# A gated MLP on one Trainium2 core: raw weight rows of the down projection fetched two steps sooner and, in the first pass, ahead of the last three stores, with loads of sums and of the next x begun later

## Chip, cores and metric

The kernel runs on one core of one Trainium2 chip. The metric is the device time of one execution in microseconds. A profiled execution also gives the span, from the first to the last instruction, which is about 2 us shorter.

## The reference

```python
# x: [1, 2048, 1024], w_gate, w_up: [1024, 3584], w_down: [3584, 1024], all bf16
g = jnp.einsum("bsd,df->bsf", x, w_gate)
u = jnp.einsum("bsd,df->bsf", x, w_up)
h = _gelu(g) * u
return jnp.einsum("bsf,fd->bsd", h, w_down)
```

## The kernel before

The 2048 rows of x are done in two passes of 1024. A pass has an up phase (14 units that produce the hidden tile `hT`) and a down projection. Both use 7 instead of 8 block products, after Winograd's form of Strassen's scheme, so the down projection needs sums of blocks of w_down as well as raw blocks. In the first pass each unit makes the sums of one row block of w_down on the side and stores them to a scratch tensor `td` in DRAM; the last unit makes three. The down projection then reads them back.

The down projection is written as numbered steps. An agenda says at which step each load is put on the queue; at each step TensorE does four or eight matmuls. All these loads and stores are issued by one engine, SP, in program order. The steps do not gate SP by time: they only fix the order of its instructions. SP waits when an instruction's data or buffer is not ready, and then everything behind it waits too.

```python
AT12 = [2, 2, 5, 5, 8, 8, 16, 18, 20, 22, 27, 29, 31, 33]   # steps of the loads of sums
...
def store_made(j):                      # 0.75 MB: three sums of row block j
    nc.sync.dma_start(out=td[:, j], in_=made[j][:, :3].bitcast(f32))
...
def load12(j):
    if j in BIG12:                      # (0, 2, 4): two blocks' sums in one 1 MB load
        big = wpool.tile([P, 2, 2, N], f32, name="w")
        nc.sync.dma_start(out=big, in_=td[:, j : j + 2, :2])
        ...
    elif j - 1 not in BIG12:            # 6 to 13: two loads of 256 KB
        ...
def fetch12(n):                         # 256 KB: one raw row tile, enough for 8 matmuls
    kh, j = n // 7, 2 * (n % 7)
    rl = slot([P, 2, N], bf16, "raw")
    nc.sync.dma_start(out=rl, in_=wdn[:, kh, j : j + 2, :N])
    raw[1, n] = rl
...
for n in range(NJ):                     # NJ = 14
    at(max(-1, 2 * n - 6), fetch12, n)
...
# down projection, phase one: steps 0 to 27, four bf16 matmuls each
for kh in range(2):
    ...
    for j in range(NJ):
        step(kh * NJ + j)
        rl = raw[1, kh * 7 + j // 2]
        rows((e, c)[kh], hT[:, kh, j, 0, :], rl[:, j % 2, :], j == 0, j == NJ - 1)
# phase two reads the sums (q12), from step 28
...
# in each unit of the up phase (js: the row blocks whose sums it makes; the last unit has three)
if js:
    store_made(js[0])
for j in js[1:]:
    keep_whole(j)
...
def more(step):                         # beside the first down projection
    if step in (-1, 1):
        store_made(NJ - 2 + (step > 0))
    ...
    if step >= 16 and step % 2 == 0 and step // 2 - 8 < len(moves):
        c, ko = moves[step // 2 - 8]
        transposing(xT, c, ko, (2 * (ip + 1) + c) * N)      # the next pass's x
```

I call the fourteen tiles of `fetch12` rows 0 to 13, and "big loads" the three 1 MB loads of sums.

## Time and profile before

The median of the first three runs was 549.08 us (548.2 to 550.6). The page of the profiled execution (548.68 us, span 546.8) says what bounds it. In its lines, PE is TensorE; the digits are tenths in 40 equal slices of the span; the last line is the chain of waits that ended last, by engine.

```profile
span 546.8 us, 7414 instructions
...
PE 536.2 (98%) x2405; PEld 378.7 (69%) x2405; DVE 341.3 (62%) x526; ACT 258.4 (47%) x463; POOL 236.2 (43%) x212
...
PEclk9999999999999999999999999999999999999999
...
PE 92%; DMA 5%; SPq 2%; DVE 0%; issue 0%; ACT 0%; DVEq 0%; ACTq 0%
...
```

TensorE is busy 98% of the span at full clock, so time can be won only where it stands. Who waited for whom, TensorE alone; the columns are the sum in us, the number of waits and the longest:

```profile
engine line waited for: us in total, times, longest us
PE bank L111 <- DMA raw<-in_w_down_dram: 4.6, 4, 1.4
PE bank L494 <- DVE warm L428: 1.2, 1, 1.2
PE bank L111 <- DMA xT<-in_x_dram: 0.9, 2, 0.6
PE bank L444 <- DMA xn<-in_x_dram: 0.5, 1, 0.5
```

The three small entries belong to the first 21 us of the program. The rest is the first line: 4.6 us in four waits for raw rows. The timeline of TensorE shows where they are (start, us from the first start to the last end, operation, count; in brackets the idle time listed before the group and what ended it):

```profile
start us, us, engine line op out<-in xcount [idle before <-releaser]
...
184.45 1.97 PE L111 MATMUL bank<-t,sa 128*128 128x512 f32 x8
187.73 8.79 PE L111 MATMUL bank<-raw,hT 128*128 128x512 bf16 x40 [1.31 <-DMA raw<-in_w_down_dram]
197.88 1.89 PE L111 MATMUL bank<-raw,hT 128*128 128x512 bf16 x8 [1.35 <-DMA raw<-in_w_down_dram]
201.20 3.61 PE L111 MATMUL bank<-raw,hT 128*128 128x512 bf16 x16 [1.43 <-DMA raw<-in_w_down_dram]
205.28 10.52 PE L111 MATMUL bank<-raw,hT 128*128 128x512 bf16 x48 [0.47 <-DMA raw<-in_w_down_dram]
215.45 0.81 PE L111 MATMUL bank<-w,q 128*128 128x512 f32 x2
```

The up phase ends with the group of 184.45; then come the 112 matmuls of phase one, held before rows 0, 5, 6 and 8 (8 matmuls a row). At 215.45 phase two begins. (In some of the traces shown further on a few matmul records are missing, so that their counts add up to a little less than 112.)

Why the rows are late is told by the same stretch on SP's queue (start, us, issue, count):

```profile
171.64 1.52 SPq L261 DMA_DIRECT2D w<-in_w_down_dram  x3
181.89 0.33 SPq L280 DMA_DIRECT2D td<-m  x1
182.31 2.62 SPq L329 DMA_DIRECT2D raw<-in_w_down_dram  x3
185.03 0.45 SPq L280 DMA_DIRECT2D td<-w  x1
185.53 0.42 SPq L329 DMA_DIRECT2D raw<-in_w_down_dram  x1
186.05 1.22 SPq L280 DMA_DIRECT2D td<-w  x1
187.36 1.55 SPq L329 DMA_DIRECT2D raw<-in_w_down_dram  x1
188.96 1.29 SPq L290 DMA_DIRECT2D w<-td  x1
190.30 1.26 SPq L329 DMA_DIRECT2D raw<-in_w_down_dram  x1
...
```

SP issued nothing from 173.16 to 181.89: it stood at the store of the first kept sum, until DVE had made it. Behind that store the rows, two more stores and the three big loads alternate; the lines left out at the end go on in the same way, with the second and third big load behind rows 5 and 7. The stretch in which TensorE waits, with the share and speed of the DMA engines in the last two columns:

```profile
core 0: us, PE busy (x) PEld busy (x) DVE busy (x) ACT busy (x) POOL busy (x), PEclk, DMA share, GB/s
186.20:210.20 24.00, 19.43 (x88) 8.59 (x88) 19.04 (x30) 2.05 (x4) 0.00 (x0) 1.00 1.07 369
```

### The profile page before, as it was taken

Reading aid. Unit: us, or ns where it says so; the run is one execution under the profiler, and the core shown is the slowest. Engines: PE = TensorE matmul, PEld = TensorE weight load, DVE = VectorE, ACT = ScalarE, POOL = GpSimd, SP = SyncE. Lnnn points to the kernel's source line nnn. Section 1 sums busy time; section 2 is a strip of 40 time slices with the busy share of each in tenths; the row PEclk is TensorE's granted clock in tenths of the full one; section 3 lists DMA queues with packets and bytes.
Section 4 is the critical chain, followed back from the end, with each engine's and each line's share of the span. In section 5 each row is a group of like instructions: output and inputs, shape, how many; then the busy total and the mean of one; then the engine's idle time right before and its main releaser. Section 6 shows DMA issues by size and latency. Waiting matters only on the chain.

```text
span 546.8 us, 7414 instructions
## 1 busy us (share of the span) xinstructions
PE 536.2 (98%) x2405; PEld 378.7 (69%) x2405; DVE 341.3 (62%) x526; ACT 258.4 (47%) x463; POOL 236.2 (43%) x212
## 2 busy tenths in 40 slices
PE   8999999999999979999999999999999999999997
PEld 5477777667767635888877766776777775478885
DVE  3886766766666893585955555455555449766730
ACT  2466666566656410155445555555555551114431
POOL 0069966677774300000087777777777600000000
PEclk9999999999999999999999999999999999999999
DMA  8776666667645699999745222222222059373751
GB/s 210 168 199 174 173 180 203 197 179 208 199 146 173 229 383 289 308 197 276 263 134 135 78 79 77 78 77 79 77 78 77 0 199 381 133 230 97 226 187 49
DMA packets 108133, 93.28 MB, mean 171 GB/s; under 512 B 17216, under 2 KB 92992, under 8 KB 108096
## 3 DMA queue, kind: packets, MB, share of 16 engines
q1 hardware_dynamic: 103936, 90.72, 56.3%
q10 hardware_dynamic: 4160, 2.10, 1.5%
q8 instruction: 19, 0.31, 0.2%
q14 instruction: 18, 0.15, 0.1%
HBM read 74.45 MB, written 15.20 MB: 164 GB/s over the span
## 4 chain that ended last, share of the span: by engine, by line
PE 92%; DMA 5%; SPq 2%; DVE 0%; issue 0%; ACT 0%; DVEq 0%; ACTq 0%
PE bank L111 92%; DMA raw<-in_w_down_dram 3%; SPq L448 2%; DMA xT<-in_x_dram 1%; DMA xn<-in_x_dram 1%; DVE m L90 0%; SPq L437 0%; ACT bank L269 0%; ACT st L408 0%; SPq L280 0%; ACT u L107 0%; DVEq L90 0%; SPq L329 0%; ACTq L107 0%
## 5 line engine op out<-in xcount | busy, mean ns | idle before, releaser
L93 POOL TENSOR_TENSOR s<-w 128x512 fp32r<-128x512 bf16 x100 | 117.0, 1190 | 191.6 <-DVE t L90 92.8
L111 PE MATMUL bank<-t,s 128*128 128x512 f32 x648 | 157.0, 398 | 0.0
L111 PEld LDWEIGHTS bank<-t,s 128*128 128x128 f32 x648 | 121.8, 188 | 27.7
L111 PE MATMUL bank<-xT,w 128*128 128x512 bf16 (+1 forms) x504 | 116.5, 377 | 0.9 <-DMA xT<-in_x_dram 0.9
L107 ACT COPY p<-bank 128x512 f32<-128x512 f32 x124 | 70.4, 591 | 96.7 <-PE bank L111 96.7
L90 DVE TENSOR_TENSOR hT<-g,bank 128x512 bf16<-128x512 f32 x112 | 76.6, 687 | 54.7 <-ACT g L178 48.9
L111 PEld LDWEIGHTS <-w 128*128 128x128 bf16 x504 | 45.1, 98 | 60.3 <-issue 14.9
L90 DVE TENSOR_TENSOR sum<-bank,p 128x512 f32<-128x512 f32 x54 | 37.4, 692 | 53.2 <-PE bank L111 47.9
L178 ACT ACTIVATE g<-sum 128x512 f32<-128x512 f32 x81 | 51.5, 635 | 32.9 <-DVE sum L90 32.0
L111 PE MATMUL bank<-q 128*128 128x512 f32 x240 | 58.9, 389 | 0.0
L111 PE MATMUL bank<-t,sa 128*128 128x512 f32 x216 | 58.6, 413 | 0.0
L93 POOL TENSOR_TENSOR s<-w,s 128x512 fp32r<-128x512 bf16 x50 | 57.8, 1177 | 0.0
L93 POOL TENSOR_TENSOR s<-s,w 128x512 fp32r<-128x512 f32 x50 | 57.1, 1165 | 0.0
L111 PE MATMUL bank<-raw,hT 128*128 128x512 bf16 x224 | 49.2, 379 | 4.6 <-DMA raw<-in_w_down_dram 4.6
L111 PE MATMUL bank<-tb,s 128*128 128x512 f32 x216 | 53.3, 389 | 0.0
L111 PEld LDWEIGHTS bank<-q 128*128 128x128 f32 x240 | 45.1, 188 | 9.3
L111 PEld LDWEIGHTS bank<-t,sa 128*128 128x128 f32 x216 | 40.7, 188 | 10.6
L111 PEld LDWEIGHTS bank<-tb,s 128*128 128x128 f32 x216 | 40.6, 188 | 8.4
L102 ACT CAST tb<-raw 128x512 fp32r<-128x512 bf16 x28 | 17.2, 627 | 60.5 <-DMA raw<-in_w_down_dram 24.5
L107 ACT COPY u<-bank 128x512 f32<-128x512 f32 x62 | 35.9, 590 | 20.9 <-PE bank L111 19.2
L111 PEld LDWEIGHTS <-hT 128*128 128x128 bf16 x224 | 21.8, 98 | 31.6 <-issue 6.0
L90 DVE TENSOR_TENSOR bank<-bank,p 128x512 f32<-128x512 f32 x54 | 37.8, 700 | 8.2 <-PE bank L111 5.0
(44 smaller groups left out, 459.1 us busy)
## 6 DMA issues: line engine op xcount, KB each, us to landing
raw<-in_w_down_dram SPq DMA_DIRECT2D x80, 256.0 KB, 4.9
q<-td SPq DMA_DIRECT2D x60, 256.0 KB, 4.8
w<-in_w_gate_dram SPq DMA_DIRECT2D x25, 512.0 KB, 5.6
w<-in_w_up_dram SPq DMA_DIRECT2D x25, 512.0 KB, 6.5
td<-m SPq DMA_DIRECT2D x12, 768.0 KB, 4.6
w<-td SPq DMA_DIRECT2D x6, 1024.0 KB, 8.8
out_dram<-st SPq DMA_DIRECT2D x32, 128.0 KB, 1.7
td<-w SPq DMA_DIRECT2D x2, 768.0 KB, 6.7
```

The source lines that it names most:

```text
L90: nc.vector.tensor_tensor(out=out, in0=a, in1=b, op=op)
L93: nc.gpsimd.tensor_tensor(out=out, in0=a, in1=b, op=op)
L102: nc.scalar.copy(out=t, in_=src)
L107: nc.scalar.copy(out=t, in_=ps)
L111: nc.tensor.matmul(ps, lhsT=lhs, rhs=rhs, start=start, stop=stop, skip_group_check=True)
L178: nc.scalar.activation(g, src, ACT.Gelu_apprx_tanh)
L448: nc.sync.dma_start_transpose(out=xT[c][:, ko, :], in_=x2[r0 : r0 + N, ko * P : (ko + 1) * P])
```

## The change

Its intent is to bring the raw rows to TensorE in time. No compute is added or removed. Four things move on SP's queue: the last unit's store goes behind the first rows ("order"); rows are fetched two steps sooner ("sooner"); the three big loads begin 4 to 6 steps later ("sums"); and the next x begins 8 steps later ("x"). "Sooner" and "sums" change the agenda of both passes, but TensorE had no wait for rows in the second pass.

```diff
-    AT12 = [2, 2, 5, 5, 8, 8, 16, 18, 20, 22, 27, 29, 31, 33]
+    AT12 = [6, 6, 10, 10, 14, 14, 16, 18, 20, 22, 27, 29, 31, 33]
@@
-        at(max(-1, 2 * n - 6), fetch12, n)
+        at(max(-1, 2 * n - 8), fetch12, n)
@@
-                if js:
+                if len(js) == 1:
                     store_made(js[0])
@@
-            if step in (-1, 1):
-                store_made(NJ - 2 + (step > 0))
+            if step in (-1, 0, 2):
+                store_made({-1: NJ - 3, 0: NJ - 2, 2: NJ - 1}[step])
@@
-            if step >= 16 and step % 2 == 0 and step // 2 - 8 < len(moves):
-                c, ko = moves[step // 2 - 8]
+            if step >= 24 and step % 2 == 0 and step // 2 - 12 < len(moves):
+                c, ko = moves[step // 2 - 12]
```

## The prediction

> **What bounds the kernel now.** TensorE: PE is busy 98% of the 546.8 us span at full granted clock (busy table, clock row), and the chain of waits is 92% PE. After the first microseconds PE stands still for data in one place only: the start of the first down projection. The waits of PE list 4.6 us in 4 waits on the raw w_down rows: 1.31 us before 187.73, 1.35 before 197.88, 1.43 before 201.20 and 0.47 before 205.28 (timeline, 182 to 215 us). The second down projection and all other phases show no such gap. So at most 4.6 us, 0.84% of the time, can be won.
>
> **Why the rows are late.** The SP queue issues in order. Its last w_down load of the up phase ends at 173.16; then it stands 8.7 us at the store of the first kept sum, until DVE has made it (181.89). Only then do rows 0 to 2 issue; row 0 lands at 187.69, while PE is ready at 186.4. Thereafter the queue is full: from 186.4 to 216.0 it moves 364 GB/s at full DMA share (windows), and three 0.75 MB stores and three 1 MB loads of sums stand between the rows, each 2 to 3 us of queue. A 256 KB row alone takes 0.65 to 0.75 us of it. Rows landed 5.4 us after issue at first, 10.7 in the thick of it. Landings come in the order of issue, as the Trainium skill says of descriptors on one ring (DMA: Bandwidth & Descriptors, Queues, rings and completion order); the trace agrees.
>
> **What the change moves.** No instruction is added or removed; the compute engines keep their order. On SP four rows now stand before the first of the three stores, and rows 4 and 5 between them; the three big loads of sums come after rows 7, 9 and 11 instead of 4, 5 and 7. The buffers of rows 0 to 3 are those of before; their last readers, by the timeline, end between 171.8 and 175.7, so I expect issues from 173.2 to about 177 and landings (4.5 to 5 us after, as the loads of 169 to 173 show) by 182, in a time in which DMA is idle. Stacking the rest at the paces above (estimate from the landings of before), row 4 lands near 188 (needed 193.5), row 8 near 197 (200.6), row 10 near 201 (204.2), row 12 near 205 (207.8), row 13 near 207 (209.5): each tile feeds PE 1.78 us, and the slack stays above 2 us. All four gaps should go.
>
> **Given back.** The next x begins 8 steps later, so two transposes (1.14 us of SP each) now stand before the next weights at about 249 us. Those weights landed at 255.6 and 257.2, and DVE used them at 259.4, held by PE; slack about 1 to 2 us after the delay. If used up, DVE's stores push PE's fourth phase: perhaps 0.5 us.
>
> **Predicted.** 549.1 - 4.5 = 544.6 us, range 543.3 to 546.8. Faster by over 2%: 0.01; within 2%: 0.98; slower: 0.01.
>
> **What would show it.** Waits of PE: no or nearly no entry for raw rows; first raw matmul near 186.4 instead of 187.73, phase one 24.9 us instead of 29.6 long, everything later 4.5 us earlier with PE busy unchanged. Rows 0 to 3 issued before 178. No new PE gap around 255 to 265.
>
> **What would make it wrong.** A row buffer freed later than I read, holding the queue at row 1 or 2 and with it the stores; the loads of sums landing after 211 us; the late transposes holding up weights or sums; a gap hidden under another wait (banks freed by DVE at 186) that remains when the rows come early.

## The result, and the profile after

The changed kernel took 543.35 us (median of 4 runs, 542.67 to 543.71). Beside it the kernel before took 549.5 us (4 runs, 548.2 to 550.6; the three runs told of above are among them). A ratio in this document is the mean time of one kernel's runs over that of the other's of the same rounds, so not quite the ratio of the medians: here 0.9887, with a 95% interval of 0.9862 to 0.9912. That is 6.2 us of 549.4, where 4.5 had been forecast. Taken on the 549.08 us that the prediction started from, it is 542.9 us, 0.4 us below the lower end of its range.

The page after, the same lines (span, engines, granted clock, chain):

```profile
span 541.5 us, 7420 instructions
...
PE 535.2 (99%) x2405; PEld 378.0 (70%) x2405; DVE 341.6 (63%) x526; ACT 258.1 (48%) x463; POOL 236.5 (44%) x212
...
PEclk9999999999999999999999999999999999999999
...
PE 95%; SPq 2%; DMA 1%; issue 0%; ACT 0%
...
```

The waits of TensorE after:

```profile
engine line waited for: us in total, times, longest us
PE bank L494 <- DVE warm L428: 1.2, 1, 1.2
PE bank L111 <- DMA xT<-in_x_dram: 1.1, 1, 1.1
PE bank L444 <- DMA xn<-in_x_dram: 0.2, 1, 0.2
```

The entry for raw rows is gone. TensorE's timeline runs through phase one in a single group, from 186.21, 1.5 us sooner than before, to phase two at 210.21, 5.2 us sooner:

```profile
184.39 1.97 PE L111 MATMUL bank<-t,sa 128*128 128x512 f32 x8
186.21 24.35 PE L111 MATMUL bank<-raw,hT 128*128 128x512 bf16 x112
210.21 6.04 PE L111 MATMUL bank<-w,q 128*128 128x512 f32 x25
```

SP's queue after has four rows in the stretch in which it stood before, and the stores and big loads behind more rows (the second and third big load, in the lines left out, come behind rows 9 and 11):

```profile
173.21 3.76 SPq L329 DMA_DIRECT2D raw<-in_w_down_dram  x4
181.84 0.34 SPq L280 DMA_DIRECT2D td<-m  x1
182.28 0.38 SPq L329 DMA_DIRECT2D raw<-in_w_down_dram  x1
182.74 0.91 SPq L280 DMA_DIRECT2D td<-w  x1
183.74 0.84 SPq L329 DMA_DIRECT2D raw<-in_w_down_dram  x1
184.68 1.70 SPq L280 DMA_DIRECT2D td<-w  x1
186.48 2.40 SPq L329 DMA_DIRECT2D raw<-in_w_down_dram  x2
188.93 1.26 SPq L290 DMA_DIRECT2D w<-td  x1
...
```

The same 24 us window. The DMA engines move as much as before, but TensorE is now busy in all of it:

```profile
186.20:210.20 24.00, 24.00 (x113) 10.91 (x113) 19.07 (x31) 2.05 (x4) 0.00 (x0) 1.00 1.01 368
```

Three lengths make the comparison exact. "Start" is the time of the last matmul start of the up phase; "phase one" runs from there to the first matmul start of phase two; "rest" runs from there to the end of the last compute instruction (a ScalarE copy; the span ends 2.8 us after it with semaphore instructions).

| us | start | phase one | rest |
|---|---|---|---|
| before | 186.04 | 29.41 | 328.53 |
| after | 185.98 | 24.23 | 328.50 |

So the whole difference of these two traces is 5.2 us in phase one. The start of the program moved between 185.0 and 186.4 us over all fourteen profiles, with no relation to the variant: the first loads take a little more or less. That is chance that the span carries.

### The profile page after: what moved, and what is told of

Same layout as the page of the kernel before. It is cut to its first block, busy times and chain, and to the rows that moved or that the text cites. A ratio compares the mean times of both kernels' runs of the same rounds, so it can differ in the third digit from the quotient of the medians.

```text
span 541.5 us, 7420 instructions
## 1 busy us (share of the span) xinstructions
PE 535.2 (99%) x2405; PEld 378.0 (70%) x2405; DVE 341.6 (63%) x526; ACT 258.1 (48%) x463; POOL 236.5 (44%) x212
## 4 chain that ended last, share of the span: by engine, by line
PE 95%; SPq 2%; DMA 1%; issue 0%; ACT 0%
PE bank L111 95%; SPq L448 2%; DMA xT<-in_x_dram 1%; SPq L454 1%; SPq L437 0%; ACT st L408 0%
## 5 line engine op out<-in xcount | busy, mean ns | idle before, releaser
L90 DVE TENSOR_TENSOR q<-hT 128x512 fp32r<-128x512 bf16 x56 | 38.4, 686 | 4.2 <-PE bank L111 4.2
```

Source lines behind the costliest of these rows:

```text
L90: nc.vector.tensor_tensor(out=out, in0=a, in1=b, op=op)
```

## The experiments

Three questions were open. Where do 5.2 us come from when the waits list 4.6? Where does the rest of the 6.2 come from? And which part of the change is worth what? Each run below was timed in five rounds against the kernel before. This table collects the measurements; the sections say what follows. "Listed" and "waits" are the idle time and the number of TensorE's waits for raw rows. "Standstill" is phase one minus 24.23, its length in the changed kernel. "Latest row" is the row with the largest lateness, as defined below. Each phase one is that of a single profile.

| kernel | ratio to before (95%) | phase one | standstill | listed, waits | latest row, late by |
|---|---|---|---|---|---|
| before, first profile | | 29.41 | 5.18 | 4.57, 4 | 8, 5.20 |
| before again | 0.9998 (0.9977 to 1.0019) | 29.45 | 5.22 | 4.60, 4 | 8, 5.24 |
| order only | 0.9985 (0.9963 to 1.0008) | 28.53 | 4.30 | 3.82, 3 | 8, 4.31 |
| sums only | 0.9991 (0.9967 to 1.0014) | 28.16 | 3.93 | 3.31, 4 | 13, 3.94 |
| sooner only | 0.9990 (0.9969 to 1.0012) | 28.96 | 4.73 | 4.10, 4 | 9, 4.74 |
| x only | 1.0012 (0.9998 to 1.0026) | 29.76 | 5.53 | 4.91, 4 | 8, 5.54 |
| all but order | 0.9946 (0.9928 to 0.9963) | 26.06 | 1.83 | 1.69, 1 | 0 and 13, 1.84 |
| all but sums | 0.9947 (0.9932 to 0.9962) | 26.40 | 2.17 | 1.84, 2 | 9, 2.18 |
| all but sooner | 0.9936 (0.9920 to 0.9953) | 26.14 | 1.91 | 1.28, 4 | 13, 1.92 |
| all but x | 0.9911 (0.9895 to 0.9927) | 24.23 | 0 | 0 | 13, -0.64 |
| order and sums | 0.9943 (0.9931 to 0.9956) | 25.95 | 1.72 | 1.39, 2 | 13, 1.73 |
| the change again | 0.9902 (0.9888 to 0.9915) | 24.23 | 0 | 0 | 13, -0.32 |
| all but sooner, small loads later | 0.9915 (0.9900 to 0.9930) | 24.64 | 0.41 | 0.25, 1 | 11, 0.42 |

In every one of these profiles the rest was 328.50 to 328.53 us: nothing after phase one answers to the change.

### The kernel before, once more

No edit.

> The kernel of before, unchanged. The change saved 5.3 us of span but 6.2 us of time over four runs. Theory R (the queue-bound waits of before differ from run to run, and the profile of before caught a short one): the spans of these runs scatter by 1 us or more, their median is about 547.4, and the new profile's waits of PE for raw rows again come in 3 to 5 pieces but sum to something other than 4.6 us, with the span moving with that sum. Rival N (the before-runs differ in fixed cost outside the span, or by chance): spans within 0.4 us of 546.8, ratio to before 1.000, waits of PE for rows 4.6 us again.

It took 548.36 us (5 runs, 547.79 to 548.87) beside 548.07 for eleven other runs of the same kernel. The waits were again four and again 4.6 us, though differently shared out: 1.80, 0.85, 1.51 and 0.45. The spans of its five runs were 545.9 to 547.0. So theory R, that the standstill itself varies and the first profile caught a short one, gets no support here: the sum repeats to 0.04 us. (The x-only kernel below shows that it can vary by 0.35.) Rival N is nearer: the median span is 546.5, where R expected 547.4. Both had parts wrong: N expected all spans within 0.4 of 546.8, and they scatter by 1.1 us, as R said; the start moves by as much.

### One part alone: order

```diff
-                if js:
+                if len(js) == 1:
                     store_made(js[0])
-            if step in (-1, 1):
-                store_made(NJ - 2 + (step > 0))
+            if step in (-1, 0, 2):
+                store_made({-1: NJ - 3, 0: NJ - 2, 2: NJ - 1}[step])
```

> Only the last three stores moved behind the first rows. Theory Q (one queue, in order, about 0.67 us per 256 KB; what counts is how many bytes stand ahead of each row): rows 0 to 2 land by 181, so the first wait (1.3 us) goes, but the early loads of sums still stand ahead of rows 5 and 6: about 2.5 to 3.2 us of true standstill remain of 5.2, so 2.0 to 2.7 us faster, ratio about 0.996. Rival S (the queue blocked behind the store is the whole cause): all waits for rows go, ratio 0.989 as with the whole change. Accounting theory P (a PE wait costs its listed idle time plus about 0.16 us, because a matmul's modelled end is 0.38 us after its start while the next may start after 0.216): the span differs from the changed kernel's by listed waits + 0.16 per wait.

547.31 us, ratio 0.9985: less than I expected (2.0 to 2.7 us). The trace shows 0.9 us. TensorE's timeline of this run:

```profile
186.65 8.81 PE L111 MATMUL bank<-raw,hT 128*128 128x512 bf16 x39
197.31 1.89 PE L111 MATMUL bank<-raw,hT 128*128 128x512 bf16 x8 [1.86 <-DMA raw<-in_w_down_dram]
200.71 3.61 PE L111 MATMUL bank<-raw,hT 128*128 128x512 bf16 x15 [1.51 <-DMA raw<-in_w_down_dram]
204.78 10.52 PE L111 MATMUL bank<-raw,hT 128*128 128x512 bf16 x47 [0.45 <-DMA raw<-in_w_down_dram]
```

The first wait, 1.31 listed before, is gone. But row 5 now waits 1.86, where it waited 1.35, because all three stores and the first big load stand ahead of it as before. TensorE comes to row 5 sooner and waits there for part of what it no longer waits for at row 0. Rival S, that the blocked queue is the whole cause, falls. Theory P, a wait's cost, was put down as a difference of spans; as the start moves by 1 us, I tested it on phase one instead (below).

### One part alone: sums

```diff
-    AT12 = [2, 2, 5, 5, 8, 8, ...]
+    AT12 = [6, 6, 10, 10, 14, 14, ...]
```

> Only the three big loads of sums begin later (after rows 6, 8 and 10, behind the stores as before). Theory Q: the first wait for row 0 (1.3 us listed) stays, since the store still blocks; the waits at rows 5, 6 and 8 go or shrink below 0.5 us each in total under 1 us: 3.0 to 3.7 us faster, ratio about 0.994. Rival S: the store is the cause, so nothing is won, ratio 1.000. P: span difference to the changed kernel is listed waits plus 0.16 per wait.

547.74 us, ratio 0.9991; phase one 1.25 us shorter, again well under the 3.0 to 3.7 expected.

```profile
187.36 19.15 PE L111 MATMUL bank<-raw,hT 128*128 128x512 bf16 x86 [1.37 <-DMA raw<-in_w_down_dram]
207.01 1.89 PE L111 MATMUL bank<-raw,hT 128*128 128x512 bf16 x8 [0.50 <-DMA raw<-in_w_down_dram]
209.56 1.89 PE L111 MATMUL bank<-raw,hT 128*128 128x512 bf16 x7 [0.66 <-DMA raw<-in_w_down_dram]
212.22 1.89 PE L111 MATMUL bank<-raw,hT 128*128 128x512 bf16 x8 [0.78 <-DMA raw<-in_w_down_dram]
```

The waits of rows 5, 6 and 8 are gone, as expected, and row 0's stays. What I had missed stands at the end: new waits before rows 11, 12 and 13. These rows stand behind the same stores and big loads as before and, beside them, behind small loads and transposes; they land at the same time as before (row 13 at 212.2, before at 212.7). Before, TensorE came to them so late that they were there.

### One part alone: sooner

```diff
-        at(max(-1, 2 * n - 6), fetch12, n)
+        at(max(-1, 2 * n - 8), fetch12, n)
```

> Only the fetches are two steps sooner; stores and loads of sums stay. Theory Q: one row moves ahead of each store or load; row 0 still waits 1.3 us, waits near rows 6, 7 and 9 remain: about 4 us of true standstill of 5.2, so 0.8 to 1.5 us faster, ratio about 0.998. Rival S2 (the lead of two steps is what the change wins by): ratio 0.989 to 0.992. P: as before, span difference is listed waits plus 0.16 per wait.

548.1 us, ratio 0.9990; phase one 0.45 us shorter, waits at rows 0, 6, 7 and 9. The expectation of 0.8 to 1.5 us was too high, its picture right. Rival S2 falls. The 0.45 us is hardly more than the 0.35 by which the next run differs from the kernel before for no reason of its edit.

### One part alone: x

```diff
-            if step >= 16 and ... step // 2 - 8 < len(moves):
+            if step >= 24 and ... step // 2 - 12 < len(moves):
```

> Only the next x begins later. Theory Q: its first transpose stood behind row 12, long after the last wait (row 8), so phase one stays 29.4 us with the same four waits, ratio 1.000. Rival (transposes compete with rows): phase one 28.9 us or less.

548.88 us, ratio 1.0012. Phase one was 29.76, the same four waits, 0.35 us longer than in the first profile. The edit cannot be the cause: SP's instructions in the two traces are the same, in the same order, up to row 11, and the latest row is row 8. So the standstill of one and the same queue order varies by 0.35 us. This part wins nothing by itself. The four singles together make 0.88 + 1.25 + 0.45 - 0.35 = 2.2 us of the 5.2, 2.6 without the last. Their effects do not add.

### All but order

> The whole change except that the three stores stay where they were. Phase one (from the last matmul of the up phase to the first of the second down phase) took 29.4 us before, 24.2 after, and everything after it 328.5 us in all six profiles so far. Theory Q (queue order and bytes ahead of each row): row 0 is still blocked by the first store, so one wait of 1.3 to 1.8 us listed at row 0 and no other; phase one 25.7 to 26.3 us; 3.1 to 3.7 us faster than before, ratio about 0.994. Rival D (one part of the change is decisive and the others idle): equal to before or to the changed kernel within 0.4 us.

545.16 us, ratio 0.9946. One wait, at row 0, 1.69 us listed, and no other:

```profile
187.62 24.34 PE L111 MATMUL bank<-raw,hT 128*128 128x512 bf16 x109 [1.69 <-DMA raw<-in_w_down_dram]
211.61 4.71 PE L111 MATMUL bank<-w,q 128*128 128x512 f32 x19
```

Phase one is 26.06, within the expected 25.7 to 26.3. Since this wait alone pushes TensorE 1.8 us back, rows that would have been late later in the phase (row 13 by 1.84 us) are there in time.

### All but sums

> The whole change except that the big loads of sums start at their old steps. Theory Q: no wait at row 0; one or two waits at rows 7 and 9 (or 6 and 7), true standstill 0.9 to 2.5 us; phase one 25.1 to 26.7 us, ratio about 0.993. Rival D: 24.2 or 29.4 us.

545.72 us, ratio 0.9947. Two waits, 1.34 at row 7 and 0.50 at row 9, phase one 26.40: as expected.

### All but sooner

> The whole change except that rows are fetched at their old steps. Theory Q: rows 0 to 2 early, row 3 behind the first store; only the last two rows are tight: true standstill 0 to 1.0 us, phase one 24.2 to 25.2 us, ratio 0.989 to 0.991. Rival D: if the sooner fetch is decisive, 27 us or more.

544.7 us, ratio 0.9936. Phase one 26.14 against an expected 24.2 to 25.2: a miss. The waits are 0.36, 0.47, 0.23 and 0.21 at rows 9, 11, 12 and 13. One cause is in the landings: the first big load landed 3.8 us after the row before it, where the prediction had counted 2 to 3 us for such a load; everything behind it came that much later. So the sooner fetch is worth 1.9 us when the other parts are there, though 0.45 alone.

### All but x

> The whole change except that the next x starts at its old step. Theory Q: one transpose (about 0.5 us of queue) more stands ahead of row 13, which had 2 us of slack: no wait for rows, phase one 24.2 us, ratio as the whole change (0.989 to 0.991 here). Rival: the transposes hold the queue 2 us each at issue and the last row waits, 0.5 us or more of standstill.

543.6 us, ratio 0.9911, phase one 24.23, no wait for rows: the x part of the change is not needed for its gain.

### The change once more

> The changed kernel, unchanged, on another day's chip. Phase one was 5.2 us shorter in the two profiles, and the rest of the program was the same to 0.03 us in ten. Theory N (the first timing's 6.2 us held 5.2 us of standstill and about 1 us of chance, because the four runs of before had a median of 549.5 where 22 later ones had 548.1): ratio 0.990 to 0.992, 4.4 to 5.4 us. Rival R (unprofiled runs of before stand longer than profiled ones, so the whole 6.2 us is real): ratio 0.987 to 0.9895.

542.81 us (4 runs, 542.59 to 544.06) beside 548.52 (9 runs): ratio 0.9902, 5.4 us, in the range of theory N. Its interval is 0.9888 to 0.9915, and its lower part lies in the range of rival R, so this run alone does not exclude R. In four later batches the kernel before had medians of 548.07, 548.09, 548.52 and 548.25 us (40 runs in all); in the first timing it had 549.5 over 4 runs. The changed kernel had 543.35 and 542.81. So the 6.2 us of the first timing contain about 1 us that did not come again. (Against these 40 runs, most of them of other batches, the eight runs of the changed kernel are 5.2 us shorter by the medians.)

### Order and sums together

> Stores behind rows and sums later, but rows at their old steps and x at its old step. Theory Q, corrected by the run without the sooner fetch (phase one 26.1, waits at rows 9, 11, 12 and 13): the same waits, with two q loads and a transpose more ahead of rows 12 and 13: phase one 26.1 to 27.2 us, ratio 0.994 to 0.996. Rival D (order and sums together are the whole gain): 24.2 us.

545.23 us, ratio 0.9943, phase one 25.95, a little better than expected: two waits, 0.62 and 0.77 listed, at rows 12 and 13 only. Rival D falls here as in the leave-outs: without any one of order, sums and sooner, 1.7 to 2.2 us of standstill stay. (The last run shows that another edit can nearly take the place of "sooner".)

### One rule put to a test

By now the table suggested a rule. An unhindered TensorE starts the first matmul of phase one 0.23 us after the last matmul start of the up phase, takes 1.727 us for each row (8 matmuls, 0.216 us from start to start), and starts 0.04 us after a landing that it waits for; all three are read from the traces. Call a row's lateness its landing minus the landing that such a TensorE would need. In all profiles up to here the standstill was the largest lateness of the fourteen, to within 0.02 us, whenever that lateness was positive. The rule follows by arithmetic if the three figures are fixed; what the traces show is that they are.

The expectation below was written with 1.714 us for a row, from 24.0 us for 112 matmuls. That is too little: the first matmul of phase two is recorded 0.03 us after the last one of phase one, so that only 111 intervals are inside the 24.0. Its lateness values are therefore up to 0.17 us above those of the table, and its rule needed a correction of 0.1, which the right pace does without.

The kernel for the test is all but sooner, with the small loads of sums moved behind the last row:

```diff
-    AT12 = [6, 6, 10, 10, 14, 14, 16, 18, 20, 22, 27, 29, 31, 33]
+    AT12 = [6, 6, 10, 10, 14, 14, 22, 22, 24, 24, 27, 29, 31, 33]
```

> The kernel without the sooner fetch (phase one 26.1 us, standstill 1.9), with the eight small loads of sums 6 to 9 moved behind the last row. Theory M (the standstill of a phase is the largest lateness of any one of its 14 rows, landing minus the time at which an unhindered TensorE would need it, whatever the other rows do; in 13 profiles it was that less 0.1): in the kernel without the sooner fetch rows 9, 11, 12 and 13 were 0.64, 1.30, 1.70 and 2.09 us late; taking 2 and 4 loads of 0.7 us from in front of rows 12 and 13 leaves row 11 the latest at 1.30, so standstill 1.2 us (0.8 to 1.5), phase one 25.4 us, 0.7 us better and no more, though 2.8 us of queue were taken from in front of row 13. Rival A (the standstill follows the bytes in front of the last row): standstill 0, phase one 24.2 us.

543.89 us, ratio 0.9915.

```profile
186.20 19.17 PE L111 MATMUL bank<-raw,hT 128*128 128x512 bf16 x88
205.62 5.34 PE L111 MATMUL bank<-raw,hT 128*128 128x512 bf16 x24 [0.25 <-DMA raw<-in_w_down_dram]
```

There is one wait and it is at row 11, as the rule said, although row 13 had been the latest; rival A expected none. The amount is outside my range: 0.41 us of standstill instead of 0.8 to 1.5. The rule itself held (row 11 was 0.42 late); the landing that went into it was off. In the other run row 11 was 1.16 late by the table's reckoning, because the first big load took 3.0 us of queue in this run and 3.8 in the other. Why that load takes 3.0 in one run and 3.8 in another was not settled. That the later small loads took 1.5 us off the 1.91 us of standstill of "all but sooner" also shows that "sooner" is one way among others to clear the queue ahead of the last rows.

## Why the prediction was right or wrong

**What bounds the kernel, and where.** Right. TensorE stood only in phase one, and after the change it does not stand there: no wait for rows, phase one from 186.21, everything later earlier, busy time 536.2 and 535.2. All four gaps went, as predicted.

**The order of issues and landings.** Right in the main: rows 0 to 3 issued from 173.2 to 177.0 and landed by 180.5. Landings stayed in the order of issue in every trace (looked at from 168 to 222 us of each). The Trainium skill does not promise this: it says that descriptors are consumed in ring order on each DMA engine, but that completion is not first in, first out for an issuing engine (DMA: Bandwidth & Descriptors, Queues, rings and completion order).

**The step that failed: "So at most 4.6 us, 0.84% of the time, can be won."** The mechanism was right; the term was mis-sized. The true standstill was 5.2 us, 29.41 minus 24.23. The listed idle time of an engine counts from the end of its last instruction, and a matmul's end is not when the next could start. In the trace a bf16 matmul of phase one lasts 0.379 us, while matmuls start every 0.216 us where nothing holds them. So each wait hides 0.379 - 0.216 = 0.163 us by this sum; in the eleven profiles that have such waits, standstill minus listed time was 0.14 to 0.17 us for each wait. For the kernel before the sum gives 4.57 + 4 x 0.163 = 5.22, and 5.18 was measured. The Trainium skill says that a matmul's reported end is computed by the profiler and not observed (Perfetto Trace Analysis, Tensor Engine Instruction), and that a single warm matmul lasts (398 + N)/2.4 ns (TensorE: Matmul & The Clock Gate, Single matmul latency), 379 ns for N = 512, as this trace has it. I read the idle column as if it were the loss. The same reading stands in "PE is ready at 186.4": in the changed kernel the first row started at 186.21.

**The remaining microsecond of the first timing.** The two traces do not hold it: their phase one and rest account for 5.2 us, their starts differ by 0.06, and the two profiled executions took 548.68 and 543.71 us, which is 5.0. Repeated, the gain was 5.4 us, with 4.7 to 6.1 in its interval. So I put about 1 us down to chance in the first runs of the kernel before (549.5 then, 548.1 to 548.5 later). That is inferred and not shown. One rival cannot be excluded: two later runs with a lower granted clock, 0.993 and 0.997, took 549.35 and 551.21 us, 2.0 and 3.1 us more than the medians of the same kernels in their batches, and the clocks of the first four runs were not kept. Of the 1.7 us by which the measured 542.9 lies below the forecast of 544.6, the mis-sized term makes about 0.6; the rest was bad luck or is open. With 5.2 in place of 4.6 and the same width, the range would have begun near 542.7.

**"The slack stays above 2 us."** Wrong, without cost. Row 13 landed at 208.06 and was needed about 208.6: 0.6 us of slack, and 0.3 in the second profile. Two terms were off: a row feeds TensorE for 1.73 us and not 1.78, and rows 10, 12 and 13 landed about 1 us later than the estimate. The change works with little to spare.

**"Given back."** Right that it would be small: the next weights landed at 251.6 and 253.4 and DVE took them at 254.1, 0.7 us to spare, and the rest is 328.50 as before. A smaller thing was not foreseen: the time outside the span (time minus span of each run) is 1.9 us in the kernel before and 2.2 in the changed one. By the medians it was 1.9 in all kernels with neither "sooner" nor "x", 2.0 to 2.1 in the two with "sooner" but not "x", and 2.1 to 2.2 in all with "x" but the last test, which had 1.9. So the change gives back some 0.3 us there, and "x", which gained nothing in phase one, seems to bring most of it; the cause was not looked into.

**Why the parts do not add.** The rule of the largest lateness explains it. The test bore it out in place; its size was forecast wrong, through the landings. Before, row 0 was 1.5 us late, row 8 5.2 and row 13 4.1. "Order" mends row 0 and leaves row 8 at 4.3; "sums" mends row 8 and leaves row 13 at 3.9; "sooner" takes one place in the queue from each. Of the kernels run here, only those with all three have every row in time.

## What to carry to other kernels

When a stream feeds an engine, work out each piece's lateness against an unhindered consumer; the largest one is the loss, and a change that mends some pieces only moves the wait to the next. Judge the loss by start-to-start times, not by the listed idle time, which on TensorE leaves out about 0.16 us at each wait of this kind. And when the expected effect is under 1%, find a length in the trace that does not carry the chance of the program's start: here phase one of the kernel before agreed to 0.04 us in its two profiles (0.35 with the x-only kernel, whose queue is the same up to the latest row), and that of the changed kernel to less, where times scattered by 1 us and more.

## What the Trainium skill lacked or had wrong

- TensorE: Matmul & The Clock Gate, Back-to-back issue gap: it gives about 131 ns for each matmul of N = 512 in a sustained stream of weight loads and matmuls, and calls 216 ns the isolated gap that over-counts. Phase one is such a stream at full clock, without waits after the change, and its matmuls start every 216 ns (215 or 216 in 110 of its 111 intervals). So here the figure called isolated is the one that holds.
- Perfetto Trace Analysis, Tensor Engine Instruction: it says that a matmul's end is estimated, but not what that does to idle time: 0.14 to 0.17 us of real standstill missing at each wait.
- No page that I read has how the cost of a 1 MB load varies in a full queue: the first of the three landed 2.6 to 3.9 us after the landing ahead of it over the fourteen traces (3.09 before, 3.63 after, 3.82 and 2.96 in two kernels without the sooner fetch), the second and third 2.6 to 3.0.
